# A scheduled attention and mixing kernel: a new order of the same operations, and two warm-up matmuls placed earlier

## The chip, the cores and the metric

The kernel runs on one core of a Trainium2 chip. The metric is the device time of the whole program in microseconds (us). A core has a matmul engine (PE, with its weight loads listed as PEld), a vector engine (DVE), a scalar engine (ACT), a general engine (POOL), and a queue (SP) from which this kernel issues all its DMAs.

## What is computed

Four batches of 768 positions go through block-sparse attention with 8 heads of 64 columns: each query sees its neighbours at a distance under 16 and 24 summaries of blocks of 32 keys (the largest key, the mean value). The 512 output columns of a position then go through a rotation by an angle that they set themselves, two 768x768 mixes over positions, and a 512x512 channel product:

```python
k_sum = k.reshape(B, H, nb, block, D).max(axis=3)
v_sum = v.reshape(B, H, nb, block, D).mean(axis=3)
scores = concat(where(abs(i - j) < 16, scale * q @ k.T, -1e9), scale * q @ k_sum.T + log(32))
x = softmax(scores) @ concat(v, v_sum)            # (4, 768, 512) after the heads are joined
theta = x @ w_theta
zr, zi = x * cos(theta), x * sin(theta)
u = x + w_tok_r @ zr + w_tok_i @ zi               # over positions, per batch
out = u + maximum(u @ w_ch, 0)
```

The weights arrive as 8-byte floats and are turned into 4-byte floats on the chip by integer operations on DVE.

## The kernel before

`attn_moe` records 2292 operations (a few instructions each) with their readers and writers; nothing is decided while they are recorded. `Program.schedule` then walks the table `ORDER`: each word is the number of an operation, and a letter behind it (`d` DVE, `g` POOL) says on which engine it goes, where it may go on several; without a letter it goes to the engine with the smallest cost. The instructions are issued in this one order, so the table sets the order on every engine's queue and on SP, and the waits follow from the data. Every engine works its own queue in order and waits where its next instruction's data or buffer isn't there.

The parts that are spoken of below, with their lines:

- Warm-up (`K["WARM"]`, lines 374 to 379): five matmuls of a 128x512 tile of zeros into the bank `t`, whose result nobody reads. In the trace each is two pieces of L379.
- `prepass` (L446, L450): block maxima of the keys (`ks`, DVE) and, in batch 0, the value sums as matmuls of a 0/1 table with the loaded values (`x<-vn`) into `pa` on PE.
- `att_tile` for each of 24 tiles of 128 positions (6 in a batch): loads of the queries `q` (two buffers), the keys `k`, the values `v` (four buffers), scores (L523, `s`), mask and maximum (L559, DVE), exponentials (L563, ACT), transposes (L572), copies of these (L578), the value product (L546, `pa`), and the division by the sum (L587 to L596).
- `turn_tile` and `theta_tile`: a transpose (L605) and the product with `w_theta` (L639 in the first batch's six tiles, L644 later), both in the one bank `t`; the angle is reduced on ACT and DVE (L655, L657), turned into cosine and sine on ACT (L667, L668), and multiplied with `xn` in two halves (L674, on DVE or POOL, `zu`).
- `mix_step` (L702, batches 0 and 1) and `mix_fast` (L817, batches 2 and 3, seven products instead of eight; four of them read sums of weights that `weight_sums` has put into `s_scratch`, loaded by `wt<-s_scratch`).
- `out_batch` (L922 and the lines around it): the channel product, in seven products again.

Exponential and sine stand in different tables of ACT; where one follows the other, an ACT_TABLE_LOAD is issued between them.

```python
for word in ORDER.split():
    o = self.ops[int(word.rstrip("padg"))]
    o.eng = dict(p="PE", a="ACT", d="DVE", g="POOL").get(word[-1]) or min(o.cost)
    order.append(o)
```

Of the kernel before, what the change touches and what calls it, by code (L numbers as in the profile page):

```python
# [54 lines left out]
17g 8 0g 1g 31 23 27 25 9 24 18 29 10 28 2 26 39 3 19 32 30 20 4 44g 33 5 6g 190g 49g 46 45 48 7 50 86 194g 47 193 51 60 61 34  # L55
35 52 53 79 191 64 239g 192g 87 57 55 62 54 66 13 88 65 185 11 93 14 42 238 63 89 12 36 241g 40 90 59 58 240g 91 100 67 56 80
195 37 38g 235 68 15 92d 188 186 81 69 107 21 82 204 94 71 205 206 108 41g 43d 70 83 209 290 207 95g 187 72 109 84 237 210 196
208 199 76 295g 198 73 197 294g 200 189g 74 77 22 242 203 96 101 75d 102g 201 202 78d 236 251 252 351g 254 212 211 103 213 97
253 104 85 98 215 214 110 223 216 296g 258 224 99d 225 243 255 257 217 118 348g 226 105 227 218 119g 220d 293 256 245 219d 106
244 246 228 247 250 111 120 221 291 121 249 222d 248 123 124g 297 229 122 349g 298 345 259 230 260 262 292 299 261 270 130 125  # L60
301 350g 115 300 271 263 126 272 303 423g 305 302 304 306 273 267d 308 131g 307 116 264d 419 310 135 268 309 265 274 313 127
136g 132 311 312 266d 141 275 269d 314 276 133 315 142g 137 317 316 277 138 352 143 112 231 325 326 318 232 134 327 163 233g
139 144 353 361 168 319d 356 328 320 329 362 278 330 322 355 234 169g 145 331 346 164g 321d 279 364 323 363 282 117 146 324
283 420 332 354 113 347 284 280 365 474 285 147 380 358 114 357 339 165 360 148 366 359 337 166 367 338 149 167 170 368 150
152 381 424 369 422 333 370 400 153 382 128 383 384 171 334 154 172 155 157 281 158g 156 425 385 371 402 401 159 372 386 340
174 335 175g 373 426 392 394 374 421 160 375 377 376 378 387 529 161 404 176 388 379 403 705g 389 454 177 530 179 395 393 178
180 455 456 390g 472 408 457 181 405 182 410 183 427 703 458 459 414 466 409 412 460 461 462 463 411 435 428 467 429 704g 406
437 706g 438 415 431 430 441 468 615g 469 413 436 434 464g 707 521 442 433 465 432 416 417 407 479g 440 564d 523 443 439 480
288g 741 709g 534 444 446d 418 481 535 482 445 485 483 447 490 477 129 492 491 484 475 448 478g 493 486 496 449 451d 532 710g
452 743 450d 488 531g 522 453d 497 616g 487 536 509 537 539 494 586 476d 540 489 538 495 498 510 621 499 391g 501 543 500d 541  # L70
742 511 502 512 545 503 506 513 542 547 551 504 546 733 507 583 289g 286g 708g 549 505d 550 533g 343g 548 544 745 508d 514 744
552 553 515 341 554 555 524 516 556d 517 711 712 518 287g 713d 714 739 585 336g 557 344g 398 734 587 596 558d 599 519 624 588
603 559 715 592 589 716 746 717 561 668 568 591 562 565g 622 735 593 718 566 719 584 560d 597 140 601 720 595 563 598 567 600
602 399g 784 590 594 623 342 569 785d 604 473g 721 786 740 605 572 625 607d 570 634 606 576 608 626 635 787g 617 788 653g 722
618 665 638 151 789 629 574 697 637 630 396d 397g 470 619 525g 723g 737 639 627 790 698g 609d 620 636 628 520 832 612 633 736
471g 162 641 833g 654g 659g 613 738 834g 631 791 640 610 611d 632 792 614d 655 841 642 747 752 643 835g 669 526 644d 793 645
670 646 812 678 672 657 679 650 813d 671 173 667 683 681 658 814d 815 680 663 647d 836 673 748 842 816 675 664 684 843g 817
656 648 818 755 754 724 945g 837 674 682 844 819 660g 677 661 649d 651 666 527d 652 676 685 820 686 687 794 839 689 821 688d
795 838g 756 1015 757 690 528g 571 845g 975 765 662 822 759 760 976d 850 691 840 977d 578 846 978 851g 796 768 823 727d 763
184 797 852 946 699 766 758 692 853g 769 1020 701 694d 979 940 702 980 700 941 847g 772 848 693d 579 981 825 767 695 749 696d  # L80
761 762 771 731 753 750 764 580g 798d 824 982 728 770 732 773 983 774 775d 984 947 956 581g 776 854g 777 995 948 729 778d 959
849 781d 949 950 958 725g 582g 802 952 803 996 997 998 953 799g 859 751 943 1016 1021 779 951 782 855 999 730 780 1074 1000
985 860g 1001 856 800 726 963 1018 808 857 1002 942 954 861g 957 961 960 962 801 955 575 826g 783 964 862 863g 1077 858 944g
965 1003 1022 966 1004 986 967d 864g 968 1005 806 804 1017g 810 1031 972 868 805 865g 1050 828 1023 1051d 1052 1032 869g 573
577 987 829 1170 1053 830 1024 866 1025 1033 989g 1006 969d 1054 827 1035 1037 831 1029 1055 870 1028 993 871 1056 1007g 970
872g 1027 1034 867 973 1120d 1038 1008 877 994 1036 1026 1057 1019d 1058 1013 1030 971 1014 974d 873d 1059 1039 874g 1040 1042
1078 878 1041d 809 811 990g 1079 1043 1047d 1208 1076 807 1087 1089 991 876 992 1209 1088 1090 1011 1210d 1083 1094 1093 1044d
1060 879 1009 880 1211 1080 1212 875 881 1082 1129 1012 1045 882g 1048 1213 886 1061 1126 1081 1092 1066 883 1075 1010 884
1084 1091 1214 1063g 1085 887 1067 885 1062 1127 1121 1046d 988 888 1215 1086 1173 1068 1049 1216 895 1095 1096 1098 1106g
1130 1217 1097d 889 1099 1218d 1279 1107g 1280 1281g 1069 1131 1070 896 1071 1228 1133 1100d 1282 1064g 1219 1135 890 1103d  # L90
1229 1283 1072 1073 1139 1065 891g 1137 1132 1110 1141 892 1142 1101 1284 1111 897 1143 1104 1285 1134 1138 1102d 898g 1108
1105d 1145 899g 1146 1286 1140 1144 1136 1109 1287 1128 893 900d 1158d 1147 1148 901g 1150 894 1288 1172 1250 1149d 1118 1174
1289 1114 1175 1112 1151 1305 1116 1178 1179 902 1202 1236 1122 1152 1183 903 1221g 1123 1306 1124 1185 1307 1308g 1187 1177
1181 1309 1153 904 1182 1160 1184 1232 1310 1155 1189 1237 1230 1233 1220g 1188 1176 1125 1186 1311 905 1156 1162 1171 1290
1312 906g 1249 1154 1163 1203 1247 1190 1180 1157 1234 1313 1159g 1191 1192 1193 1291g 1231 1251 1314 1222g 1194d 907 1315d
1252 1254 1195 1235 1292g 1117 1354 1240 1196 1253 1355 1260 1261 1356 1161 1199d 1255 1357g 1166 1168 1319 1197 1358 1198d
1322 1256 1257 1241 1258 1164d 1165g 1169 908g 1316 1263 1242 1200 913 1359 1206 1264 1360 1259 1207 1201d 1243 909 1324 1361
1167 1262 1248 1317g 1267 1382 1599g 1266 1268 1265 1362 1269 910g 1325 1326 1363 1271d 911 1364d 1270 1327 1272 16 1368 1600g
1335 1238 1204 1226 1330 1369d 914g 1328 1463 1370d 1365 915 1387 1276 1371 1366 1205 1367g 912 1273d 1331 1334 1372 1224 1338
916 1595g 1373 1225 1274 1337 1239 1383 1587g 1374 1223 1329 917 1385 1275 1244 918g 919 1245 1293 1596g 1277 1375 1376 1227  # L100
1278 1377 1588g 1333 1388 1320 920 1332 921 1589d 1246g 1339 1294 1297 1321d 1384 1378d 1417 931 1336 1295 1342 1296 1418 1341
1419g 1323 1420 1389 922 1672 1340 1593 1301 1594 1113 1119 1343 923g 1590 1318g 1344 1644 1346 932g 1421 924g 1345 1302 1646
# [1020 lines left out]
```

## Time and profile before

| | |
|---|---|
| time, median of 3 runs | 435.23 us (433.77 to 435.77) |
| the profiled execution | 437.3 us, its span 435.6 us |
| PE busy | 421.7 us, 97% of the span |
| DVE, ACT, POOL busy | 81%, 64%, 48% |
| DMA | 100.07 MB, mean 230 GB/s |
| the chain of work that ended last | PE 87%, DMA 10%, DVE 1%, ACT 1% |

Busy time is read as time in which an instruction of the engine is under way. The span runs from the first instruction to the last; 1.7 us of the profiled execution lie outside it.

### The profile page before, as it was taken

Reading aid. Unit: us, or ns where it says so; the run is one execution under the profiler, and the core shown is the slowest. Engines: PE = TensorE matmul, PEld = TensorE weight load, DVE = VectorE, ACT = ScalarE, POOL = GpSimd, SP = SyncE. Lnnn points to the kernel's source line nnn. Section 1 sums busy time; section 2 is a strip of 40 time slices with the busy share of each in tenths; the row PEclk is TensorE's granted clock in tenths of the full one; section 3 lists DMA queues with packets and bytes.
Section 4 is the critical chain, followed back from the end, with each engine's and each line's share of the span. In section 5 each row is a group of like instructions: output and inputs, shape, how many; then the busy total and the mean of one; then the engine's idle time right before and its main releaser. Section 6 shows DMA issues by size and latency. Waiting matters only on the chain.

```text
span 435.6 us, 10044 instructions
## 1 busy us (share of the span) xinstructions
PE 421.7 (97%) x3682; PEld 350.9 (81%) x3682; DVE 352.2 (81%) x947; ACT 280.3 (64%) x600; POOL 209.7 (48%) x208
## 2 busy tenths in 40 slices
PE   5989999998999999999999999999999989999996
PEld 1455555665888888888888899999899989999996
DVE  3799999778988777875757695866489989999996
ACT  1799995787757784866785885493955447455210
POOL 3543324687775665245465578624453410251542
PEclk9899999999999999999999999999999999999999
DMA  8999956989678678848767987883379696220138
GB/s 294 347 354 364 295 197 208 290 257 322 230 233 273 197 224 266 259 139 247 232 188 223 292 273 218 245 246 119 111 230 338 229 367 223 75 73 20 65 136 289
DMA packets 76321, 100.07 MB, mean 230 GB/s; under 512 B 23024, under 2 KB 58864, under 8 KB 76272
## 3 DMA queue, kind: packets, MB, share of 16 engines
q1 hardware_dynamic: 76272, 99.43, 71.1%
q8 instruction: 29, 0.48, 0.5%
q14 instruction: 20, 0.16, 0.1%
HBM read 75.82 MB, written 23.59 MB: 228 GB/s over the span
## 4 chain that ended last, share of the span: by engine, by line
PE 87%; DMA 10%; DVE 1%; ACT 1%; SPq 0%; issue 0%; POOL 0%; DVEq 0%
PE m L702 25%; PE m L817 19%; PE t L644 11%; PE c L922 7%; PE m L922 6%; PE pa L546 5%; PE s L523 4%; PE t L639 3%; PE t L605 3%; DMA q<-qg 3%; PE pa L572 3%; DMA wth<-wth 2%; DMA wt<-wti 2%; DMA zu<-kT 2%; DMA wt<-s_scratch 1%; PE t L922 1%
## 5 line engine op out<-in xcount | busy, mean ns | idle before, releaser
L817 PE MATMUL m<-wt,hl 128*128 128x384 f32 x504 | 95.7, 339 | 1.4 <-DMA wt<-s_scratch 1.2
L817 PEld LDWEIGHTS m<-wt,hl 128*128 128x128 f32 x504 | 87.7, 188 | 4.9 <-ACT hl L309 1.5
L702 PE MATMUL m<-wt,hl 128*128 128x512 f32 (+1 forms) x432 | 84.9, 341 | 0.0
L702 PEld LDWEIGHTS m<-wt,hl 128*128 128x128 f32 x432 | 68.6, 188 | 10.8
L563 ACT ACTIVATE e<-e,st 128x118 f32<-128x118 f32 x192 | 63.1, 388 | 12.1 <-DVE st L559 11.6
L559 DVE CUSTOM_DVE_ANT_0 e<-s,cs 128x118 f32<-128x118 f32 x192 | 46.8, 272 | 9.6 <-PE s L523 4.7
L318 POOL TENSOR_TENSOR hl<-zu,hl 128x512 fp32r<-128x512 f32 x23 | 30.1, 1309 | 43.9 <-DMA wt<-s_scratch 15.9
L644 PE MATMUL t<-wth,xh 128*128 128x512 f32 x144 | 45.3, 396 | 0.0
L674 POOL TENSOR_TENSOR zu<-xn,zu 128x512 f32<-128x512 f32 x20 | 27.0, 1350 | 20.3 <-ACT zu L668 5.5
L657 DVE SCALAR_TENSOR_TENSOR zu<-zu,t 128x512 f32<-128x512 f32 x24 | 16.4, 684 | 24.4 <-ACT zu L655 24.4
L702 PE MATMUL m<-wt,zu 128*128 128x512 f32 (+1 forms) x96 | 33.4, 491 | 1.2 <-DVE zu L674 1.2
L655 ACT ACTIVATE zu<-t,bmagic 128x512 f32<-128x512 f32 x24 | 16.5, 687 | 23.9 <-PE t L644 18.3
L309 ACT CAST hl<-zu 128x512 fp32r<-128x512 f32 x31 | 19.1, 619 | 18.2 <-PE m L817 14.9
L702 PEld LDWEIGHTS m<-wt,zu 128*128 128x128 f32 x96 | 17.5, 190 | 15.8 <-issue 12.6
L546 PEld LDWEIGHTS pa<-v,e 118*64 118x64 f32 x768 | 24.8, 137 | 6.8 <-issue 3.0
L318 DVE TENSOR_TENSOR hl<-zu,hl 128x512 fp32r<-128x512 f32 x37 | 27.6, 751 | 2.3 <-ACT hl L309 2.1
L523 PE MATMUL s<-k,q 64*64 64x118 f32 x768 | 25.6, 272 | 3.9 <-POOL cs L340 3.2
L546 PE MATMUL pa<-v,e 118*64 118x65 f32 x768 | 28.1, 224 | 1.2 <-ACT e L578 1.2
L730 POOL TENSOR_TENSOR zu<-zu 128x512 f32<-128x512 f32 x15 | 21.4, 1432 | 15.0 <-DVE zu L730 4.9
L644 PE MATMUL t<-wth,xl 128*128 128x512 f32 x72 | 28.6, 397 | 0.0
L674 DVE TENSOR_TENSOR zu<-xn,zu 128x512 f32<-128x512 f32 x28 | 24.7, 884 | 4.8 <-ACT zu L668 4.6
L523 PEld LDWEIGHTS s<-k,q 64*64 64x64 f32 x768 | 20.2, 135 | 9.2 <-POOL cs L343 4.0
(181 smaller groups left out, 909.9 us busy)
## 6 DMA issues: line engine op xcount, KB each, us to landing
wt<-s_scratch SPq DMA_DIRECT2D x48, 384.0 KB, 4.4
v<-vg SPq DMA_DIRECT2D x48, 195.0 KB, 5.3
s_scratch<-f SPq DMA_DIRECT2D x24, 384.0 KB, 3.9
k<-kg SPq DMA_DIRECT2D x18, 376.0 KB, 5.5
q<-qg SPq DMA_DIRECT2D x24, 256.0 KB, 6.0
wt<-wtr SPq DMA_DIRECT2D x6, 768.0 KB, 11.0
wt<-wti SPq DMA_DIRECT2D x6, 768.0 KB, 11.4
f<-kT SPq DMA_DIRECT2D x12, 384.0 KB, 4.3
```

The lines of the kernel that those rows point to most:

```text
L309: nc.scalar.copy(dst(), src())
L318: lambda e: V[e].tensor_tensor(dst(), src(), hi().bitcast(F32), op=ALU.subtract), reads, writes, due, port=BOTH)
L523: mm(0.79 * len(pairs) / NP, [lambda p=p, g=g, h=h: nc.tensor.matmul(sc[h].get()[ROW[g], p], q.get()[ROW[h], p, ROW[g]], k.get()[ROW[h], p ...
L546: mm(2 * 0.433 + scores[0] + (0.2 if scores[0] else 0.0), [lambda n=n, g=g, a=a: nc.tensor.matmul(xa[a].get()[ROW[g], n], turned[g].get()[ ...
L559: op({"DVE": 0.205}, lambda eng, n=n: nc.vector.tensor_tensor_reduce(e()[:, n], sc[n % 2].get()[:, 2 * a + n // 2], mask(m), -SCALE, 3.0e3 ...
L563: op({"ACT": 0.288}, lambda eng, n=n: nc.scalar.activation(e()[:, n], e()[:, n], AF.Exp, bias=st.get()[:, n:n + 1], scale=-1.0), [(st, n)] ...
L644: calls = [lambda t=t, xx=xx, k=k, c=c: nc.tensor.matmul(th.get(), xx.get()[:, c], w_th[c].get()[:, k], start=(c == 0 and t == 0), stop=(c ...
L674: op({"DVE": c_dve(DM, "two"), "POOL": c_pool(DM)}, lambda e, z=z, hc=hc: V[e].tensor_tensor(z(), xn[b, i].get().rearrange("p h d -> p (h ...
L702: nc.tensor.matmul(acc[th](), zz, w[:, TT[th]], start=(s == 0 and r == 0 and t == 0 and (th == 0 or c == 0)), stop=(s == NT - 1 and r == 1 ...
L730: lambda e: V[e].tensor_tensor(dst(), x(), y(), op=ALU.add if sign > 0 else ALU.subtract), reads, writes, due, port=BOTH)
L817: calls = [lambda ref=ref, tt=tt, z=z, s=s, j=j, t=t, x=x, k=k, bank=bank, first=first: nc.tensor.matmul(bank[j].get()[:, :HT], z.get()[:, ...
L922: calls = [lambda k=k, t=t, x=x, y=y: nc.tensor.matmul(to.get(), weights[n][x][0]()[:, k, j * P:(j + 1) * P], operands[n].get()[:, y, k], ...
```

## The change

Only the table `ORDER` differs; the 2292 operations, their costs, buffers and sizes are the same, and the file after is one line shorter, so that its line numbers are one lower. 267 operations go to another engine than before (of those that may choose), and of the 548 operations on PE 208 keep their place in PE's queue while the rest move, by 21 places at most and by 1.6 in the mean.

```diff
 ORDER = """
-17g 8 0g 1g 31 23 27 25 9 24 18 29 10 28 2 26 39 3 19 32 30 20 4 44g 33 5 6g 190g 49g 46 45 48 7 50 86 194g 47 193 51 60 61 34
...
+17g 23 25 8 9 24 18 31 19 21 22 27 0 11 28 29 26 1g 2 10 3 30 44 48g 46 4 45g 32 49 39 5 47g 33 190 6 20 50 7g 51 191g 60 86
...
```

In the table, 17 is the memset of the zeros, 18 to 22 are the five matmuls on them, and 32 is the first value sum.

**PE, the start of the program.** `t<-zu` are matmuls on zeros (two of them stand as x2), `pa<-x,vt` the value sums of batch 0, `s<-k,q` the scores of tile 0. Before:

```order
L379 MATMUL t<-zu 128x512 x2
L450 MATMUL pa_107<-x,vt 24x512 x2
L379 MATMUL t<-zu 128x512
L523 MATMUL s_129<-k,q 64x118
L523 MATMUL s_131<-k,q 64x118
```

After:

```order
L378 MATMUL t<-zu 128x512 x4
L449 MATMUL pa_117<-x,vt 24x512 x2
L378 MATMUL t<-zu 128x512
L522 MATMUL s_132<-k,q 64x118
L522 MATMUL s_134<-k,q 64x118
```

Two matmuls on zeros stand ahead of the first value sums now; before they stood behind the transposes and behind the value product of tile 0. On SP the first value load `x<-vn` goes third instead of first, behind two of the four key loads.

**SP, the 25th DMA and its neighbours.** `wt` are the mixing weights, `q` the queries of tile 4, the `v` ahead of and behind it the two halves of tile 3's values. Before:

```order
L303 DMA wt<-wti 128x1536
L303 DMA wt<-wtr 128x1536
L303 DMA v<-vg 96x520
L303 DMA q<-qg 128x512
L303 DMA v<-vg 96x520
```

After:

```order
L302 DMA wt<-wti 128x1536
L302 DMA wt<-wtr 128x1536
L302 DMA q<-qg 128x512
L302 DMA v<-vg 96x520 x2
L302 DMA wt<-wtr 128x1536
```

The queries of tile 4 stand ahead of both halves of tile 3's values now.

**PE, and the engine that makes its input, at the last mix step of batch 0's first half.** `t<-wth,..` is the angle of tile 6, `m<-wt,zu` the mix of tile 5. PE before:

```order
L644 MATMUL t<-wth_972,xh 128x512 x2
L644 MATMUL t<-wth_972,xl 128x512
L702 MATMUL m_722<-wt,zu 128x512
L702 MATMUL m_704<-wt,zu 128x256
L644 MATMUL t<-wth_1011,xh 128x512 x2
L644 MATMUL t<-wth_1011,xl 128x512
L702 MATMUL m_702<-wt,zu 128x512
```

DVE before, where `zu<-xn,zu` makes the half of tile 5 that this mix reads:

```order
L588 TENSOR_SCALAR st<-pa_1271 128x4
L559 ISA e,st<-s_1296,cs 128x118
L559 ISA st 128x1
L674 TENSOR_TENSOR zu<-xn,zu 128x2x256
L559 ISA e,st<-s_1294,cs 128x118
```

PE after:

```order
L643 MATMUL t<-wth_923,xh 128x512 x2
L643 MATMUL t<-wth_923,xl 128x512
L643 MATMUL t<-wth_987,xh 128x512 x2
L643 MATMUL t<-wth_987,xl 128x512
L701 MATMUL m_686<-wt,zu 128x512
L701 MATMUL m_688<-wt,zu 128x256
L701 MATMUL m_721<-wt,zu 128x512
```

POOL after, where the row with x2 makes both halves of tile 5:

```order
L317 TENSOR_TENSOR wth_987<-xl,wth_987 128x512
L494 COPY v<-vs 24x520
L317 TENSOR_TENSOR wt<-wt 128x768
L673 TENSOR_TENSOR zu<-xn,zu 128x2x256 x2
L317 TENSOR_TENSOR wt<-wt 128x768 x2
```

The fourth group of the angle of tile 6 stands ahead of the mix now, and tile 5's product moved from DVE to POOL.

ACT's queue holds 28 table loads before and 36 after. Before, the sines of tiles 9 and 10, 16 and 17, 18 and 19, 20 and 21 shared one load; now each tile has its own, and as many loads lead back to the exponentials.

## Rows read from the trace of the kernel before

**Rows 1.** The page, part 1: engine, busy us, share of the span, instructions.

```profile
PE 421.7 (97%) x3682; PEld 350.9 (81%) x3682; DVE 352.2 (81%) x947; ACT 280.3 (64%) x600; POOL 209.7 (48%) x208
```

**Rows 2.** Stages: length, busy PE, PEld, DVE, ACT, POOL, clock, DMA share, GB/s.

```profile
40.00:100.00 60.00, 58.63 (x518) 35.43 (x510) 53.57 (x144) 50.47 (x107) 28.80 (x28) 1.00 0.81 258
100.00:160.00 60.00, 60.00 (x639) 49.42 (x639) 49.08 (x155) 42.78 (x99) 41.45 (x38) 1.00 0.75 244
160.00:240.00 80.00, 80.00 (x763) 68.30 (x762) 55.87 (x185) 55.10 (x119) 39.42 (x38) 1.00 0.75 226
...
300.00:340.00 40.00, 40.00 (x258) 37.73 (x258) 30.48 (x63) 23.33 (x51) 19.91 (x17) 1.00 0.60 201
340.00:430.00 90.00, 88.58 (x506) 87.64 (x505) 87.04 (x140) 38.35 (x64) 27.88 (x18) 1.00 0.45 154
```

**Rows 3.** Waits of PE: who waited for whom, us in total, times, longest.

```profile
PE m L702 <- DVE zu L674: 1.2, 1, 1.2
...
PE m L817 <- DMA wt<-s_scratch: 1.2, 1, 1.2
PE t L605 <- DVE zu L657: 0.7, 1, 0.7
PE s L523 <- DMA q<-qg: 0.4, 1, 0.4
```

**Rows 4.** PE in order of time at the start: start, us, what, idle before.

```profile
1.39 3.40 PE L379 MATMUL t<-zu 128*128 128x512 f32 x4 [1.39 <-POOL zu L377]
4.72 1.90 PE L450 MATMUL pa<-x,vt 128*24 128x512 f32 x4
...
10.92 1.78 PE L523 MATMUL s<-k,q 64*64 64x118 f32 x32 [3.25 <-POOL cs L340]
12.63 4.53 PE L450 MATMUL pa<-x,vt 128*24 128x512 f32 x8
17.09 1.04 PE L523 MATMUL s<-k,q 64*64 64x118 f32 x32
...
18.66 1.12 PE L379 MATMUL t<-zu 128*128 128x512 f32 x2
```

**Rows 5.** Short stretches of the start, columns as in rows 2.

```profile
10.90:12.60 1.70, 1.68 (x32) 1.43 (x32) 0.06 (x1) 0.84 (x4) 1.49 (x6) 0.56 1.03 404
14.85:17.10 2.25, 2.25 (x9) 0.43 (x7) 2.16 (x7) 2.07 (x7) 1.58 (x3) 1.00 1.06 340
```

**Rows 6.** The chain that ended last, its first 40 us: start, us, what.

```profile
18.58 9.06 DMA wt<-wti
...
27.66 11.64 DMA q<-qg
```

**Rows 7.** SP's queue, the issue ahead of that of tile 4's queries.

```profile
26.87 0.33 SPq L303 DMA_DIRECT2D v<-vg  x1
```

**Rows 8.** ACT on the way to the first mix.

```profile
41.10 0.59 ACT L309 COPY x<-t 128x512 f32<-128x512 f32 x1 [0.40 <-PE t L605]
```

**Rows 9.** ACT and DVE around the wait at 99 us, in order of time.

```profile
96.98 0.62 ACT L668 ACTIVATE zu<-zu 128x512 f32<-128x512 f32 x1
...
97.50 0.81 ACT L309 CAST wt<-wt 128x768 fp32r<-128x768 f32 x1
...
97.62 2.30 DVE L674 TENSOR_TENSOR zu<-xn,zu 128x512 f32<-128x512 f32 x1
...
98.33 1.28 ACT L563 ACT_TABLE_LOAD   x1
```

**Rows 10.** POOL in the same stretch.

```profile
96.30 1.30 POOL L674 TENSOR_TENSOR zu<-xn,zu 128x512 f32<-128x512 f32 x1 [1.58 <-DVE xl L318]
```

**Rows 11.** PE in the same stretch.

```profile
97.90 0.62 PE L644 MATMUL t<-wth,xh 128*128 128x512 f32 x2
...
99.98 1.56 PE L702 MATMUL m<-wt,zu 128*128 128x512 f32 x4 [1.23 <-DVE zu L674]
```

**Rows 12.** PE at 351 us.

```profile
351.48 1.80 PE L817 MATMUL m<-wt,hl 128*128 128x384 f32 x9 [1.20 <-DMA wt<-s_scratch]
```

More of the change, by code (lines that the diff above doesn't have):

```diff
@@ L59 @@
[L59 to L66, printed above, removed]
@@ new lines @@
+612 638 622 396d 832 727g 630 637 665 609d 629 788 618 833g 628 789 627 574 619 790 613 745 632 610 639 633 631 611d 641 744
+620 636 791 614d 728g 755 162 640 724 657 642 746 397 792 643 793 645 644d 739 669 646 678 681 812 655 834g 670 747 472 672
+673 658 666 682 835g 740 173 813 473g 841 794 659g 647d 940 471 656 814 815 679 650d 816 674 654g 677 676 817 671 667 818 648
+661 651 836g 819 685 680 663 752 748 683 675 753 649d 945g 652 686 837d 526 684 842g 687 660 795 820 688d 756 689 697 757 690
@@ new lines @@
+946 821 759 843g 975 765 691 976d 796g 838g 844 662 694d 527 528 692 839 664 701 797 699 693d 749 822 578g 702 768 845g 767
+823 766 977 763 771 769 760 978 840 846 979 764 698 731 825 943 571 850 750 579 941 758 980 981 732 751g 695 696 982 851g 852g
+762 847 848 770 761 1020 772 754 580d 700 773 983 853 824 1021 798 849 774 581g 775d 984 854g 947 776 956 777 582g 1018 995
+781d 802 958 948 949 950 957 944 959 778d 996 855g 729 859 997 1015 951 985d 856g 963 960 730 998 954 953 860g 725d 962 779
@@ new lines @@
+1059 1079 1009g 874g 807 1043 878g 1080 1087 879g 1208 1082 1047 811 1209 1084 1210 1014 880g 1090 875 876 1068 1076 886 1091
+1044d 1048 1045 1094 1211g 991 1008g 1060 1212 992 1213 1086 1083 1061 1046 1063g 1173 1089 1081 1069 881 882d 887g 1214 1049
+1010g 1011 1093 1088 1085 883g 1092 888g 1215 1012 884 1095 889g 885 1096 895 1130 1097d 1062g 1216 1098 1099 1131 1217 1103
+1279 1139 1280d 1218 1141 1104 1140 1135 1281 1072 1066 1282g 1132 1144 1067 1143 1228 1106g 890g 896g 1133 1283 1070 1120g
@@ new lines @@
+1335 1327 1276d 1370 1273d 1277 1205 913 1224 1371g 1388 1372 1274 1238 1275d 1338 1278 1337 1239 1223g 1225 1373 1364 1365
+912 1600g 1227 1385 914 1330 1329 1374 1366g 1367 1375 1244 1341 922 1331 1593d 1376 1463 923 915 1328 1377 924g 1293 1383
+1339 1333 1603g 1295 1342 1589g 1320 1336 1334 1434 1245 1340 1378 925g 916g 1417 1418 1294 1246 1389 1419d 1297 1332 1323g
+1590 917g 1343 1119 1344 1296 1420 1301 1379 1303 1345 1421 918 1422 1390 1346 1644 1681 1298 1595d 1321d 1393 1380g 1394 1423
@@ new lines @@
+1424 1347 1397 1425 1299 1594g 1645 1351 1431 1647 1391 919 1649 1386g 1658 1646 1426 1395 1648 1675 1381 1596g 1660 1398
+1348d 1384d 920 1651 1427 1352 1349 1399 1302 1662 1428 1401 1405 1350d 1650 1353d 926g 1678 1403 1400 1402 1392 1396 1404
+1429 1591g 1115 927d 1435 1592 1406 1407 1652 928 921 1653 1409 1408d 1611 1597 1654 931 1436 1598 1300 1410 1411 1672 1604g
+1527 1304 1664 932g 1437 930 1656 929 1444 1439 1430 1528 1659 1498 1529 1655 1661 1446 933 1447 1601 1663 934 1432 1530 1451
@@ new lines @@
+1580 1686 1473 1692 1619g 1701 1462 1689 1620g 1612 1540 1484 1485 1539 1499 1581 1613 1617d 1618g 1623g 1582 1486 1487d 1691
+1488 1766 1690 1627 1614g 1500 1508 1583d 1489 1767 1694 1697 1693 1511 1696 1502 1768g 1492 1493 1769 1621d 1512 1501 1699
+1504 1700 1584 1509 1704 1513 1497 1506 1770 1729 1510 1703 1771 1707 1490 1503 1622 1632 1507 1732 1491 1496 1629 1702 1624
+1625g 1505 1772 1705 1706 1494d 1735 1773 1585g 1709 1628 1514 1774 1738 1708 1586g 1515 1516 1517 1626 1775 1518 1543 1519d
@@ L141 @@
+2258 2262 2264 2282 2263 2268 2285 2265 2280 2289 2228 2283 2266 2269 2286 2284 2267 2287 2259 2270 2288 2290 2291
 """
```

136 lines of the change are left out of this document (59 added, 77 removed).

## The prediction

> **What bounds the kernel now.** First the page's list of engines: PE is busy for 421.7 of 435.6 us [rows 1], so what is left for any order to win is 13.9 us, and the question is where these lie. The table by stages gives that: from 40 us on PE has no idle slice but in two stages, 40 to 100 (58.63 of 60) and 340 to 430 (88.58 of 90); from 100 to 340 it is full in every stage shown, and this at a granted clock of 1.00 [rows 2]. PE's work is the same in both kernels, so after 40 us only waits of PE can be won, or made. The list of waits names them: 1.2 us of the mix L702 for DVE's product `zu` and 1.2 us of L817 for a load of `wt<-s_scratch` [rows 3]. Two more of that list stand before 40 us: 0.7 us of a transpose for DVE's L657, and 0.4 us of scores for a load of `q`.
>
> Before 40 us it is another program. PE waits 3.25 us ahead of its first scores [rows 4], and the loads share the 16 DMA engines at 1.03 and 1.06 of their time [rows 5]: they pace the start. The chain of waits says so too: up to 39.30 us it goes from load to load, the last one that of tile 4's queries, issued at 27.66 and landed after 11.64 us [rows 6]. That issue comes 0.02 us after the weights `wti` issued at 18.58 have landed (18.58 + 9.06 = 27.64): SP issues when an earlier load has landed.
>
> **The two matmuls on zeros.** An operation of them is two pieces. At the start four pieces took 3.40 us, 0.85 each, and behind the transposes one operation took 1.12 [rows 4], so the two taken out of there free about 2.2 us of PE between 18 and 23 us. Put in at the start they cost 4 x 0.85 = 3.40 us at most; PE there has an idle 3.25 us to fill, and ends its early work at 10.92 or at worst (1.39 + 3.40 + 3.40 + 1.90 + 1.12 = 11.21) some 0.3 us behind it. The second gain is speed. The scores that follow the idle stretch ran at a granted clock of 0.56, a mix of the two levels 1.2 and 2.4 GHz [rows 5], and took 1.78 us where the same 32 matmuls take 1.04 at 17.09; the eight pieces of value sums behind took 4.53 where four took 1.90, that is 4.53 - 3.80 = 0.73 too much [rows 4]. If PE isn't idle before, up to 0.74 + 0.73 = 1.47 us come back. So PE gains 2.2 + 1.47 = 3.7 us of room, and I count none of it: PE then waits longer for the loads of tile 2 to 4, which land when they did [rows 6]. What hides the edit is the DMA pace; the bounds are 0 and -3.7, and the row that it is nearest to is the chain's, hence 0. The first value load goes third rather than first on SP; the sums that read it now start 3 us later, so nothing is late by that.
>
> **Queries of tile 4 ahead of tile 3's values.** The issue moves from 27.66 to the place of the `v` at 26.87 [rows 6, 7], 0.79 us earlier; by bytes, one `v` of 96x520 4-byte numbers is 199.7 KB, at 340 GB/s [rows 5] an estimated 0.59 us. So PE's scores of tile 4 start 0.59 to 0.79 us earlier, more than their wait of 0.44. How much of it arrives at the first mix? The way there goes through ACT, which copies tile 4's turned columns at 41.10 and was idle for 0.40 us only ahead of that [rows 8]; the ACT work in front of the idle time hangs on weights' landings that don't move. So **-0.40**, between 0 and -0.79. The values of tile 3, delayed by one load of `q`, are read by PE behind the scores and land before them.
>
> The Trainium skill's page "DMA: Bandwidth & Descriptors" (section "Queues, rings and completion order") says that transfers issued by one engine need not complete in the order of issue; by that an earlier issue buys nothing sure, this term could be 0 and the time 434.0. In this trace the issue that follows a landing by 0.02 us speaks for the order of issue at the start.
>
> **Tile 5's product from DVE to POOL, and the angle's fourth group ahead of the mix.** ACT ends the sine of tile 5 at 96.98 + 0.62 = 97.60; DVE takes the product at 97.62 and needs 2.30 us [rows 9], to 99.92, and PE's mix starts at 99.98 after 1.23 us idle [rows 11], so that it was ready at 98.75. After the change POOL makes it. POOL's own product in this stretch took 1.30 and POOL had been idle for 1.58 us before it [rows 10]; from 97.60 it is done at 98.90. PE arrives later than before, by the group that now stands ahead (three pieces; the last such group ahead of the mix began at 97.90, so one takes 98.75 - 97.90 = 0.85) [rows 11]: 98.75 + 0.85 = 99.60. That is 0.70 us behind POOL, so the wait is gone: **-1.23**. With POOL at 2.30, as slow as DVE was, it would be 99.90, a wait of 0.30 and a gain of 0.93. The angle's group costs nothing, since it only trades places. The second half of tile 5, which POOL makes next (to 100.20), has its mix much later.
>
> **The wait at 351.** PE's queue is the same there, and so is the distance in PE's work from the issue of the `wt<-s_scratch` loads to the mix that waits [rows 12]; I leave it, 0, with bounds -1.20 (gone) and +1.20 (twice as long).
>
> **Eight more table loads.** One takes 1.28 us [rows 9]. Eight are 10.3 us of ACT, and where they stand ACT is busy for 42.78 of 60, 55.10 of 80 and 23.33 of 40 us [rows 2], that is idle for 17.2, 24.9 and 16.7 us. That is the cover: 0 on PE's path, at worst all 10.3. The 12 operations more on ACT and 11 fewer on DVE that the new letters bring go the same way; DVE, busy for 87.04 of 90 us at the end [rows 2], is relieved if anything. Elsewhere PE's moves, 1.6 places in the mean, change no work: 0, with a new wait as a rival below.
>
> The page "ScalarE: Activation LUTs" of the Trainium skill (section "What ACT_TABLE_LOAD costs") adds a drain to the load, some 2.66 us for a switch, 21 us for eight. The trace shows none: the cast ends at 97.50 + 0.81 = 98.31, the load starts at 98.33 [rows 9]. By the page the slower rival below would be twice as dear.
>
> **The sum.** -1.23 - 0.40 = -1.63 us. Made against the profiled run that is 437.3 - 1.6 = 435.7 (its span 435.6 and 1.7 us around it); that run lies 2.1 above the median of the three, so on the median: 435.23 - 1.63 = **433.6**.
>
> **Rivals.**
> 1. More is won. The wait at 351 goes with the transfers around it (-1.20), the transposes at the start no longer wait for DVE (-0.68), and the queries bring their whole 0.79 instead of 0.40 (-0.39): -2.27 beyond the forecast, 431.3. For it: all are small and hang on orders that changed. Against it: PE's order is unchanged at the first, and the other two are bounded by the loads.
> 2. A new wait of the old size. One of the products that move to POOL, where it takes 1.27 to 1.30 against 0.7 of DVE undisturbed, is what a mix of the next tiles waits for, as the mix of tile 5 did for 1.23: 433.6 + 1.2 = 434.8, the gain of the start alone. For it: 267 operations change engines, and 340 of PE's 548 change place. Against it: from 100 us on the mixes never waited for these products.
> 3. Slower: the table loads. Where a tile's sines split two runs of exponentials, the scores of the next tile wait in `e` for ACT, and PE for its transposes. If of the four pairs two lie on PE's path, four loads of 1.28, 5.1 us, are paid: 433.6 + 5.1 = 438.7; with all eight 443.9. It decides when a tile's stretch leaves ACT less than one pair (2.6 us) idle. For it: ACT is the engine whose order this change worsens most. Against it: some three tenths to two fifths of ACT's time is idle in those stages.
> 4. That the order doesn't do what it says is excluded in the queues; at the start it does it with no effect if the loads pace everything, which is the 0 already taken.
>
> **How the numbers follow.** A measurement of this kernel can tell about 0.5%, 2.2 us: faster is under 433.05, slower over 437.4. The three runs differ by 2 us, so a forecast of 433.6 lies on both sides of the first bound. Forecast (432.4 to 434.6): 0.40, of it 0.17 faster and 0.23 same. Rival 1: 0.25, of it 0.24 faster and 0.01 same. Rival 2: 0.19, of it 0.01 faster, 0.15 same, 0.03 slower. Rival 3: 0.16, of it 0.02 same and 0.14 slower. Sums: faster 0.42, same 0.41, slower 0.17. The range 430.5 to 437.5 leaves out a fifth of rival 1 (0.05), most of rival 3 (0.13) and the end of rival 2 (0.02).
>
> **What would show it.** In the profile of the changed kernel: no idle time of PE ahead of the mix of tile 5 near 98 to 99 us, POOL's L673 at 1.3 us behind the sine; the scores of tile 0 at 1.04 us and a granted clock of 1.00 at 11 us; yet the scores of tile 4 near 39 us, 0.4 to 0.8 earlier; the same wait for `wt<-s_scratch` near 350; 36 table loads with PE full from 100 to 340 us. I am wrong if PE shows idle time in that stretch with ACT as its releaser (rival 3), if a mix waits for POOL (rival 2), or if the first mix of batch 0 starts 2 us or more earlier, for then the DMA pace wasn't what bounded the start.

## The result and the profile after

The changed kernel takes 441.18 us (median of 4 runs, 439.32 to 441.72) against 435.29 us of the kernel before (433.77 to 435.77): a ratio of 1.0133, with a 95% interval of 1.0106 to 1.0160. It is slower by 5.9 us by these medians, where 433.6 and a range up to 437.5 had been forecast.

The page of the kernel after, part 1, answers to [rows 1]:

```profile
PE 422.5 (96%) x3682; PEld 350.1 (80%) x3682; DVE 353.8 (80%) x936; ACT 299.1 (68%) x629; POOL 205.6 (47%) x207
```

PE has the same work (422.5 us busy, 421.7 before), in a span of 440.0 instead of 435.6 us: the loss is waiting. Its place is read from the waits of PE of the kernel after (columns as in [rows 3]; the line numbers are one lower than before):

```profile
PE pa L545 <- ACT e L577: 2.2, 2, 1.2
PE s L522 <- POOL k L499: 2.1, 3, 1.4
PE m L816 <- DMA wt<-s_scratch: 1.6, 3, 0.9
...
PE pa L449 <- DMA x<-vn: 1.2, 1, 1.2
PE s L522 <- DVE st L558: 1.0, 1, 1.0
PE m L701 <- DVE x L720: 1.0, 1, 1.0
...
PE s L522 <- ACT f L400: 0.6, 1, 0.6
```

All of these but the L816 and L701 rows belong to the first 45 us. The mix that waited 1.23 us for tile 5's product (L702 for `zu`) is no longer in the list. Two rows of PE, the scores of tile 4 and the first mix, say when the start is over:

```profile
42.24 1.04 PE L522 MATMUL s<-k,q 64*64 64x118 f32 x32 [0.62 <-ACT f L400]
...
48.71 1.56 PE L701 MATMUL m<-wt,zu 128*128 128x512 f32 x4
```

The same two in the kernel before:

```profile
39.44 1.04 PE L523 MATMUL s<-k,q 64*64 64x118 f32 x32 [0.44 <-DMA q<-qg]
...
45.65 4.57 PE L702 MATMUL m<-wt,zu 128*128 128x512 f32 x13
```

They stood 2.80 and 3.06 us earlier. So three of the 4.4 us by which the span grew are lost in the start. Three stretches of the start, of the kernel before (first three rows) and of the kernel after (last three), columns as in [rows 2], the last two being the DMA share and GB/s:

```profile
3.00:8.00 5.00, 4.67 (x9) 0.97 (x7) 1.07 (x2) 0.00 (x0) 0.56 (x2) 1.00 1.00 369
8.00:20.00 12.00, 8.87 (x90) 3.98 (x90) 9.84 (x40) 8.56 (x22) 5.26 (x13) 0.86 1.04 368
20.00:38.00 18.00, 16.02 (x218) 9.98 (x218) 16.80 (x74) 17.38 (x45) 9.64 (x15) 1.00 1.04 344
```

```profile
3.00:8.00 5.00, 4.42 (x7) 1.54 (x5) 1.18 (x3) 0.00 (x0) 1.33 (x4) 1.00 0.93 340
8.00:20.00 12.00, 9.21 (x88) 3.27 (x90) 7.75 (x30) 6.58 (x19) 4.64 (x14) 1.00 1.04 347
20.00:38.00 18.00, 13.27 (x224) 9.05 (x219) 15.80 (x72) 15.98 (x41) 12.03 (x17) 1.00 1.03 317
```

From 8 us on the DMA engines are as full as before (1.03 to 1.04 of their time), and move less: 347 and 317 GB/s instead of 368 and 344. The chain of waits of the kernel after, in its first 45 us, goes from load to load again:

```profile
5.82 11.93 DMA wth<-wth
17.77 9.89 DMA v<-vg
27.68 13.49 DMA wt<-wtr
```

The last one is the 26th load, a block of the mixing weights; it lands at 27.68 + 13.49 = 41.17. In the kernel before the 26th load is the same block, behind the same 25 loads in another order, and it lands at 37.65. The profile puts the 0.62 us ahead of the scores of tile 4 down to ACT, which takes the first step of turning this block into floats there (L400, done at 42.11). But the scores read `k` and `q`, and the queries of tile 4, now the 27th load, are issued here:

```profile
28.48 0.33 SPq L302 DMA_DIRECT2D q<-qg  x1
```

They land at 42.11, and the scores start 0.14 us behind that, exactly as in the kernel before (landed at 39.30, scores at 39.44). So it is these queries that PE waits for in both kernels, and they come 2.8 us later although they stand one place earlier.

### The profile page after: what moved, and what is told of

It is laid out like the page before. It is cut to its first block, busy times and chain, and to the rows that moved or that the text cites. A ratio compares the mean times of both kernels' runs of the same rounds, so it can differ in the third digit from the quotient of the medians.

```text
span 440.0 us, 10050 instructions
## 1 busy us (share of the span) xinstructions
PE 422.5 (96%) x3682; PEld 350.1 (80%) x3682; DVE 353.8 (80%) x936; ACT 299.1 (68%) x629; POOL 205.6 (47%) x207
## 4 chain that ended last, share of the span: by engine, by line
PE 80%; DMA 14%; SPq 2%; DVE 2%; ACT 0%; issue 0%; DVEq 0%
PE m L701 23%; PE m L816 18%; PE t L643 9%; PE c L921 7%; PE m L921 5%; PE pa L545 5%; DMA wt<-s_scratch 4%; PE s L522 4%; PE t L638 3%; DMA wt<-wtr 3%; DMA wth<-wth 3%; PE t L604 3%; PE pa L571 2%; DMA v<-vg 2%; SPq L302 2%; DMA f<-f_scratch 2%
## 5 line engine op out<-in xcount | busy, mean ns | idle before, releaser
L816 PE MATMUL m<-wt,hl 128*128 128x384 f32 x504 | 95.6, 339 | 1.7 <-DMA wt<-s_scratch 1.6
L816 PEld LDWEIGHTS m<-wt,hl 128*128 128x128 f32 x504 | 87.6, 188 | 6.0 <-DMA wt<-s_scratch 2.5
L701 PE MATMUL m<-wt,hl 128*128 128x512 f32 (+1 forms) x432 | 85.2, 341 | 1.0 <-DVE x L720 1.0
L701 PEld LDWEIGHTS m<-wt,hl 128*128 128x128 f32 x432 | 68.4, 188 | 12.2 <-DVE x L720 1.6
L562 ACT ACTIVATE e<-e,st 128x118 f32<-128x118 f32 x192 | 64.0, 390 | 6.4 <-DVE st L558 4.6
L673 POOL TENSOR_TENSOR zu<-xn,zu 128x512 f32<-128x512 f32 x23 | 31.1, 1358 | 23.2 <-ACT zu L667 11.6
L701 PE MATMUL m<-wt,zu 128*128 128x512 f32 (+1 forms) x96 | 33.3, 491 | 0.0
L308 ACT CAST hl<-zu 128x512 fp32r<-128x512 f32 x33 | 20.1, 620 | 15.9 <-PE m L816 11.3
L317 DVE TENSOR_TENSOR hl<-zu,hl 128x512 fp32r<-128x512 f32 x38 | 30.1, 795 | 0.9 <-POOL hl L310 0.5
L577 DVE COPY e<-pa 118x512 f32<-118x512 f32 x17 | 11.7, 690 | 23.6 <-PE pa L571 23.4
L729 POOL TENSOR_TENSOR f<-f 128x192 f32<-128x192 f32 x31 | 20.0, 647 | 19.7 <-DVE f L729 9.9
L522 PE MATMUL s<-k,q 64*64 64x118 f32 x768 | 25.3, 268 | 3.8 <-POOL k L499 2.1
L701 PEld LDWEIGHTS m<-wt,zu 128*128 128x128 f32 x96 | 17.4, 190 | 13.9 <-issue 12.1
L577 ACT COPY e<-pa 118x512 f32<-118x512 f32 x31 | 17.5, 587 | 14.2 <-PE pa L571 14.2
```

The costliest lines, as they stand in the source:

```text
L308: nc.scalar.copy(dst(), src())
L317: lambda e: V[e].tensor_tensor(dst(), src(), hi().bitcast(F32), op=ALU.subtract), reads, writes, due, port=BOTH)
L522: mm(0.79 * len(pairs) / NP, [lambda p=p, g=g, h=h: nc.tensor.matmul(sc[h].get()[ROW[g], p], q.get()[ROW[h], p, ROW[g]], k.get()[ROW[h], p ...
L562: op({"ACT": 0.288}, lambda eng, n=n: nc.scalar.activation(e()[:, n], e()[:, n], AF.Exp, bias=st.get()[:, n:n + 1], scale=-1.0), [(st, n)] ...
L577: lambda e, t=t, g=g: (nc.scalar.copy if e == "ACT" else nc.vector.tensor_copy)(t.get()[:NK], tp[g].get()[:NK].rearrange("k n q -> k (n q) ...
L673: op({"DVE": c_dve(DM, "two"), "POOL": c_pool(DM)}, lambda e, z=z, hc=hc: V[e].tensor_tensor(z(), xn[b, i].get().rearrange("p h d -> p (h ...
```

## The experiments

Fourteen kernels were run. The runs of before and of each kernel were made on one chip side by side; each ratio is to the before of its own group (medians 435.28 to 435.44). A ratio is taken over the runs that are compared and is not the quotient of the two medians; the two can differ by 0.1% (`weights_first`: 1.0037 and 1.0048), so that the intervals decide. Nearly every kernel here is a table `ORDER` put together from the two tables, so that the diffs show words of the table, cut to those that move.

### Which part of the program loses it

`before_start` takes the table of before up to the first mix, then what is left in the order of after; `after_start` the other way round.

```diff
 before_start
-(all words of before)
+(the first 295 words of before) (the other words, as they follow in after)
 after_start
-(all words of before)
+(the first 284 words of after) (the other words, as they follow in before)
```

> The order of the kernel before up to the first mix of batch 0 (its first 295 table entries), the rest in the order of the kernel after. Theory (the loss is made at the start, by loads that move fewer bytes in a microsecond: the scores of tile 4 start at 42.24 instead of 39.44): the first mix starts near 45.65 as before, the +3.05 us of the start are gone, what the rest makes by PE's waits is -1.4 (tile 5's product) +1.4 (L701 at 114 us) +0.9 (L816 at 296) -0.1 (351), so 435.3 + 0.8 = about 436.1. Rival (the loss is in the later waits): 438 to 440.

> The order of the kernel after up to the first mix of batch 0 (its first 284 table entries), the rest in the order of the kernel before. Theory (the start makes the loss): the first mix starts near 48.7, 3 us late, the rest keeps its waits, 435.3 + 3.0 = 438.3. Rival (later waits): within 1 us of 435.3.

`before_start`: 436.29 us, ratio 1.0029 (1.0008 to 1.0049). `after_start`: 438.72 us, 1.0088 (1.0065 to 1.0112). The two parts make 1.0117 together, within the interval of the whole change (1.0106 to 1.0160); three quarters of these 1.17% are the start. The PE rows of `before_start` (first two) and of `after_start`:

```profile
38.51 1.04 PE L523 MATMUL s<-k,q 64*64 64x118 f32 x32 [0.78 <-DMA q<-qg]
44.74 5.43 PE L702 MATMUL m<-wt,zu 128*128 128x512 f32 x16
```

```profile
41.87 1.04 PE L523 MATMUL s<-k,q 64*64 64x118 f32 x32
48.09 2.42 PE L702 MATMUL m<-wt,zu 128*128 128x512 f32 x6
```

### The kernel before once more

> The kernel before, unchanged, for its spread. If the speed of the loads at the start differs from execution to execution, the packets of the values (2080 bytes, median 118 ns between 20 and 40 us in the first profile of before, 147 in that of after) and the start of tile 4's scores (39.44) differ here by more than 1 us from the first profile; the theory that the order decides expects them within 0.5 us, and a ratio of 1.000 +- 0.002.

435.21 us, ratio 0.9994 (0.9976 to 1.0012). Its profiled execution had the scores of tile 4 at 38.72 (39.44 in the first profile), the 26th load at 37.39 (37.65), and 335 GB/s between 20 and 38 us (344). So two executions of one order differ by 0.7 us at this place; the two of after's start, 42.24 and 41.87, lie 2.4 to 3.5 us behind both. The expected 0.5 us was too narrow, the theory stands. A second thing differs by execution: the wait for `wt<-s_scratch` at 351 us. It was 1.20 us in the profile on which the prediction rests [rows 12]; here PE shows none:

```profile
343.71 8.56 PE L817 MATMUL m<-wt,hl 128*128 128x384 f32 x44
352.49 0.76 PE L817 MATMUL m<-wt,hl 128*128 128x384 f32 x3 [0.22 <-DVE x L826]
```

### The two matmuls alone

```diff
-... 3 19 32 30 20 ... 21 ... 22 ...
+... 3 19 21 22 32 30 20 ...
```

(18 to 22 are the matmuls on zeros, 32 the first value sum.)

> The kernel before with the two matmuls on zeros moved ahead of the first value sums and nothing else. Theory (the order of the loads makes the loss, the matmuls are in PE's idle time): the scores of tile 0 at 1.0 to 1.2 us instead of 1.78, the first mix within 0.5 us of 45.65, 435.3 +- 0.7. Rival (the matmuls delay the start themselves): the first mix 1 to 3 us late, 436.3 to 438.3.

435.68 us, ratio 1.0016 (1.0001 to 1.0031): at most a small loss. In its profiled execution, the longest of its twelve (437.79 us), the scores of tile 0 took 1.33 us (1.78 in the first profile, 1.36 in that of `before_again`), those of tile 4 began at 39.61, the first mix at 45.83. What names the change in its headline is not what costs the time.

### The order of the loads alone

`before_loads_after` is the kernel before with its first 29 loads in the order of after; `after_loads_before` is the kernel after with its first 29 loads in the order of before.

```diff
-31 23 27 25 29 39 33 86 35 79 185 93 42 40 100 235 188 186 107 108 290 109 237 236 110 111 291 345 292
+23 25 31 27 29 39 33 86 35 79 185 42 40 93 100 235 107 186 188 108 290 109 237 236 110 111 345 291 292
```

(31, 29 and 33 are the first values, 23 to 27 and 39 keys and queries, 86, 79, 93 and 100 `wth`, 42 and 40 the halves of tile 0's values, 188 and 186 those of tile 1, 107 and 108 the first blocks of `wtr` and `wti`, 345 the queries of tile 4, 291 and 292 the values of tile 3.)

> The kernel before; only the first 29 loads are issued in the order of the kernel after (the same 29 loads), every other engine keeps its order. Theory A (the order of the loads makes the start slow: the third block of weights of wtr, the 26th load in either order, lands at 41.17 in after, 37.4 to 38.2 in three executions with the start of before): that landing near 40, the scores of tile 4 near 41.5, 435.3 + 2 to 3 = 437.3 to 438.3. Rival B (the order of ACT, DVE and POOL at the start makes it slow, and the loads follow, since an issue waits for buffers): the scores of tile 4 at 39 to 40, 435 to 436.

> The kernel after; only its first 29 loads are issued in the order of the kernel before. Theory A: the scores of tile 4 come back to 39 to 40, 441.2 - 2 to 3 = 438 to 439 or lower. Rival B: they stay near 42, 440.5 to 441.5.

`before_loads_after`: 439.19 us, 1.0085 (1.0051 to 1.0119). `after_loads_before`: 436.53 us, 1.0031 (1.0008 to 1.0054). The order of 29 loads, with nothing else changed, makes as much as the whole start (1.0088), and with the old order of loads the kernel after loses no more than it does with the whole old start. The stretch from 20 to 38 us, and in a fence of its own the row of the scores of tile 4, of `before_loads_after` (first two fences) and of `after_loads_before` (last two):

```profile
20.00:38.00 18.00, 14.04 (x210) 8.91 (x212) 15.11 (x66) 14.66 (x36) 7.81 (x13) 1.00 1.04 331
```

```profile
43.09 1.04 PE L523 MATMUL s<-k,q 64*64 64x118 f32 x32
```

```profile
20.00:38.00 18.00, 16.46 (x199) 10.18 (x194) 16.99 (x72) 16.95 (x45) 10.07 (x16) 0.91 1.03 351
```

```profile
38.60 1.04 PE L523 MATMUL s<-k,q 64*64 64x118 f32 x32
```

The landings of three loads in the traces, in us from the start of the span, say where the time goes. The sets of loads up to each are the same in all kernels (`weights_first` and the others below are the single moves):

```
order of the loads         kernel               11th    16th    26th
before                     before               16.5    22.7    37.6
                           before_again         15.6    21.2    37.4
                           before_start         15.7    20.9    37.1
                           warm_only            16.1    21.6    38.2
                           after_loads_before   15.2    20.0    36.6
after                      after                18.6    23.6    41.2
                           after_start          17.3    21.5    39.5
                           before_loads_after   18.7    24.5    41.7
before, one move           weights_first        15.4    20.0    37.5
                           values_early         15.5    20.1    36.8
                           keys_first           15.9    22.1    38.7
                           q4_first             15.3    20.0    36.8
```

The executions profiled of `after`, `before_loads_after` and `warm_only` were the longest of their kernels; that of `after_start` (438.98 us) stands in the middle of its six, and its 26th load still lands 1.4 us behind the latest of the old order. One thing holds in all 16 traces: none of the 9th to the 30th load is issued before the load eight places ahead of it has landed, and most of them 0.02 to 0.08 us behind that. So a load that lands late also delays the issue eight places on, and in this way the order of the first loads reaches the later ones.

### The moves one by one

```diff
 weights_first
-235 188 186 107 108
+235 107 188 186 108
 values_early
-185 93 42 40 100
+185 42 40 93 100
 keys_first
-31 23 27 25 29
+23 25 31 27 29
 q4_first
-111 291 345 292
+111 345 291 292
```

> The kernel before with one load moved by two places: the first block of wtr goes ahead of the two halves of tile 1's values instead of behind them (loads 17 to 19), as in after. The 17th to 19th load together took 3.1, 4.0 and 4.4 us from landing to landing in three executions with the start of before, 4.8 and 5.6 us in two with that of after. Theory A in its narrow form (this group makes half of the loss): the three take 5 us or more and the scores of tile 4 start 1.0 to 1.5 later than in before, 436.3 to 436.8. Rival: 3.5 to 4.4 us, and 435.3 +- 0.5.

437.38 us, ratio 1.0037 (1.0012 to 1.0063). The three loads took 5.3 us and the scores of tile 4 came at 40.30, 0.9 us behind the first profile and 1.6 behind `before_again`, about as theory A expected, but the way there was another: the 26th load is not late (37.5), and these scores don't wait for their queries, which land at 38.84. What is late are the values themselves: with 768 KB of weights ahead of them they land at 24.6 and 25.3, where the later half came at 24.1 in before and 22.5 in `before_again`, and PE's value product of tile 1 waits for them. First of the waits of PE:

```profile
PE pa L546 <- DMA v<-vg: 2.2, 1, 2.2
```

In this execution the wait has a second price. Behind it the granted clock of PE is 0.51 from 26.0 to 29.4 us, nearly all of that at the lower of its two levels (1.2 GHz instead of 2.4). The value product and the matmuls behind it, here and (last two rows) in the kernel before, where PE had waited 0.66 us and the clock was 1.00:

```profile
25.44 1.76 PE L546 MATMUL pa<-v,e 118*64 118x65 f32 x32 [2.20 <-DMA v<-vg]
27.12 2.08 PE L639 MATMUL t<-xh,x 128*128 128x512 f32 x2
```

```profile
25.70 1.22 PE L546 MATMUL pa<-v,e 118*64 118x65 f32 x32 [0.66 <-ACT e L578]
26.85 1.13 PE L639 MATMUL t<-xh,x 128*128 128x512 f32 x2
```

From the start of the value product to the third of these pairs PE takes 4.60 us instead of 2.97, so that the slow stretch costs 1.6 us on top of the wait. Not every wait is followed by one: in `keys_first`, below, PE waits 1.67 us and its scores then take 1.04 us as always.

> The kernel before with the two halves of tile 0's values loaded 12th and 13th instead of 13th and 14th, ahead of a block of wth, as in after. Theory (values beside a large block make the loads slow): the 11th load lands 0.7 to 1.3 us later than the 15.1 to 16.5 of the runs with before's loads, the 26th near 38, 435.3 + 0.5 to 1. Rival: nothing, 435.3 +- 0.4.

435.94 us, 1.0020 (1.0005 to 1.0035): the time is in the expected band, the reason isn't: neither the 11th nor the 26th load is late. The execution profiled is the shortest of its twelve (435.41 us), so where the loss lies isn't seen.

> The kernel before with the first two loads of keys ahead of the first load of values, as in after. In two executions of the start of after the third load landed 2.4 to 3.4 us behind the second, in seven with before's loads 1.1 to 2.4. Theory (this place costs about 0.6 us, since all loads follow one another): 435.3 + 0.6. Rival (the third landing varies by itself): 435.3 +- 0.4.

437.87 us (median of seven runs; an eighth, 441.89, is not in the ratio), 1.0055 (1.0030 to 1.0081), and widely spread, 435.21 to 439.77. Much dearer than the 0.6 us expected. The first value sum waits for its values (first row), and the queries of tile 4 are late (second row, the scores of tile 4); the chain of waits up to these goes through loads alone:

```profile
7.36 1.88 PE L450 MATMUL pa<-x,vt 128*24 128x512 f32 x4 [2.19 <-DMA x<-vn]
...
40.28 1.04 PE L523 MATMUL s<-k,q 64*64 64x118 f32 x32 [1.67 <-DMA q<-qg]
```

The profiled execution (436.97 us) is among the faster ones of this kernel, so that what its slower ones do isn't seen.

> The kernel before with one load moved by one place: the queries of tile 4 go ahead of the first half of tile 3's values, as in after. This is the term of the prediction that was put at -0.40 (between 0 and -0.79). By the prediction: these queries land 0.6 to 0.8 earlier against the 26th load, 434.9. By the theory that has come out of the runs (a load's place changes the speed of the loads around it): the values of tile 3 stand side by side then, the loads around lose what the queries gain, 435.3 +- 0.4.

435.63 us, 1.0000 (0.9986 to 1.0013). In the trace the queries of tile 4 land 0.8 us behind the 26th load, where in the other executions of the old order they land 1.2 to 1.7 behind it: they are earlier by 0.4 to 0.9 us, as forecast. Their scores start at 37.68 and the first mix at 44.40, which is hardly outside what the old order shows by itself (37.96 to 39.61 and 44.22 to 45.83). By time no gain of the 0.4 us forecast can be told from none.

In time the first three moves make 0.37 + 0.20 + 0.55 = 1.12%, the whole order 0.85% (0.51 to 1.19): they are enough for it. That their losses add up in this way isn't shown: part of that of `weights_first` is the lower clock, and the granted clock of the kernel after is 1.00 from 8 to 38 us. By landings they don't add up: the 26th load lands at 39.5 to 41.7 with all moves and at 36.8 to 38.7 with any one. Why they slow the loads more together than alone stays open.

### Is it the place of the values in memory?

```diff
-dma(lambda g=g: v[g].get()[NB:], lambda g=g: vg[b, 2 * i + g], ...
+dma(lambda g=g: v[g].get()[NB:], lambda g=g: vg[b, 2 * i + g][:, :H * DV].rearrange("p (h d) -> p h d", h=H), ...
...
-vg = np.zeros((B, NG, VL, H, DV), np.float32)
+vg_rows = np.zeros((B, NG, VL, 640), np.float32)
```

> The kernel before with the values stored in rows of 2560 bytes instead of 2080, of which 2080 are loaded as before. The packets of the values (2080 bytes) take 85 ns at best, 118 to 132 in the median between 20 and 40 us, and the packets of the weights beside them (6144 bytes) rise from 234 to over 300. If this comes from the place of the rows in memory, both fall towards 85 and 235 here, the start is paced less, and the time is 432 to 434. If it comes from where the rows are written or from the number of rows (96 for 16 engines), nothing changes: 435.3 +- 0.5.

435.47 us, ratio 0.9992 (0.9973 to 1.0011): no change by itself. In the trace a packet of the values takes 112 ns in the mean between 8 and 38 us here, 120 and 129 ns in the two executions of before, 146 in that of after; 85 is its least. Rows 2560 bytes apart don't bring the packets back to that, so their place 2080 bytes apart is not what slows them.

### Tile 5, and the late waits, alone

```diff
 tile5_only
-... 344g ... 519 ... 568 ... 718 566 ...
+... 519g 344g ... 718 568 ... 566 ...
 late_only
-(all words of before)
+(the words of before up to PE's 304th operation) (the other words, as they follow in after)
```

(519 is the product of tile 5, 344 a subtraction on POOL, 718 the angle's last group, 568 the mix.)

> The kernel before with two changes near 98 us and none elsewhere: the half of tile 5's product that the mix waits for goes on POOL, ahead of a subtraction (L318) that POOL does there, and the last group of the angle of tile 6 stands ahead of that mix. Theory (this term of the prediction was right): the wait of 1.23 to 1.26 us ahead of that mix is gone, 435.3 - 1.2 = 434.1. Rival (something later swallows it): 435.3 +- 0.4.

434.80 us, ratio 0.9982 (0.9962 to 1.0002). PE ahead of the mix, in `before_again` (first row) and in `tile5_only` (the angle's last group and, with no idle time, the mix):

```profile
99.18 1.56 PE L702 MATMUL m<-wt,zu 128*128 128x512 f32 x4 [1.24 <-DVE zu L674]
```

```profile
97.78 0.62 PE L644 MATMUL t<-wth,xh 128*128 128x512 f32 x2
98.23 0.40 PE L644 MATMUL t<-wth,xl 128*128 128x512 f32 x1
98.47 1.88 PE L702 MATMUL m<-wt,zu 128*128 128x512 f32 x5
```

The wait is gone; of the 1.2 us the medians show 0.6, and the interval just reaches no gain. In the traces PE is 1.5 us ahead of `before_again` behind this mix, loses 0.4 of it near 106 us and 0.2 near 142, and keeps 0.9: the rival, that something later swallows the gain, is right in part.

> The order of the kernel before up to PE's 304th operation (some 265 us), the rest in the order of the kernel after. The kernel with before's start and after's rest ran 436.3 although the wait at tile 5 is gone from it, so that some 2 us are lost behind. Theory (PE's waits near 283 and 345 to 352 us, for the loads of the sums and DVE, make this loss): 435.3 + 1.5 to 2.5 = 436.8 to 437.8, waits of 0.5 us or more near 283 and 1 us or more near 350. Rival (it is lost between 100 and 265 us): 435.3 +- 0.5.

436.15 us, 1.0012 (0.9996 to 1.0027): less than expected, and not sure to be a loss. The trace has the waits near 350 that were expected (two of 0.9 us), and none near 283:

```profile
345.74 4.94 PE L817 MATMUL m<-wt,hl 128*128 128x384 f32 x27 [0.91 <-ACT hl L309]
351.57 1.68 PE L817 MATMUL m<-wt,hl 128*128 128x384 f32 x8 [0.89 <-DMA wt<-s_scratch]
```

The order of after behind the start costs 1.0029 although it has the gain at tile 5 in it; what makes this is settled only in part: some of it lies here, the rest in small waits that differ from run to run.

### What helped, together

```diff
-the words of before, rows of 2080 bytes
+the words of tile5_only, rows of 2560 bytes
```

> The kernel before with the two changes near 98 us (tile 5's product on POOL, the angle's last group ahead of the mix) and with the values in rows of 2560 bytes. If both small effects are real (0.9982 and 0.9992 alone), 435.3 x 0.9974 = 434.2; the rows alone were within their interval of no change, so 434.2 to 434.8.

434.17 us, ratio 0.9967 (0.9952 to 0.9983): faster than both kernels, by 1.2 us and by about 7. The interval overlaps that of `tile5_only` (0.9962 to 1.0002), so what the rows add to it isn't shown.

## Why the prediction was wrong, step by step

- **Tile 5's product, -1.23: right.** In the kernel after POOL begins the two halves 0.07 us behind the sine (99.92 + 0.62 = 100.54), and the mix follows the angle's last group without idle time. Rows of ACT, POOL and PE of the kernel after, answering to [rows 9 to 11]:

```profile
99.92 0.62 ACT L667 ACTIVATE zu<-zu 128x512 f32<-128x512 f32 x1
...
100.61 2.83 POOL L673 TENSOR_TENSOR zu<-xn,zu 128x512 f32<-128x512 f32 x2 [3.42 <-ACT zu L667]
...
102.23 2.31 PE L701 MATMUL m<-wt,zu 128*128 128x512 f32 x6
```

Here the kernel after makes up 1.5 us of its lateness in the traces (2.94 us late ahead of this stretch, 1.44 behind it). Alone it is worth 0.6 us by the medians (0.9982, with 1.0002 at the end of the interval).

- **The order of the loads, -0.40: this is the step that failed.** I costed one moved load, the queries of tile 4, and took the others to land when they did. Three more had moved: keys ahead of the first values, tile 0's values ahead of a block of `wth`, a block of weights ahead of tile 1's values. Put together the order of the 29 loads costs 1.0085, some 3.7 us, and in the kernel after the queries of tile 4 land at 42.11 instead of 39.30 and their scores come 2.80 later, not 0.4 to 0.8 earlier. Two sentences of the prediction hold the mistake: that the loads "land when they did", and that the first value sums "now start 3 us later, so nothing is late by that"; in the kernel after they wait 1.2 us for `x<-vn` (in the list of waits above), and `keys_first` shows what this move costs alone, 1.0055. The profile had shown that the loads pace the start; the conclusion should have been that every change of their order is a change of the path, and that each moved load has two prices: that of what it delays, and that of the rate at which the loads around it run.

- **The queries' own term** was sized well by the landings: alone the queries land 0.4 to 0.9 us earlier against the 26th load. It doesn't show in the time (1.0000). The Trainium skill's page "DMA: Bandwidth & Descriptors" (section "Queues, rings and completion order"), which was weighed there, says that completion need not follow the order of issue. No trace here shows such a case: in all 16 the first 30 loads landed in the order of issue.

- **The two matmuls on zeros, 0: nearly right.** Alone 1.0016, at most a small loss. The 0.74 us of slow scores that I thought could come back was a matter of one execution: at a granted clock of 1.00, `before_again` had 1.36 us for them with the matmuls at their old place and 1.90 us of idle time ahead.

- **Eight more table loads, 0: right as far as can be seen, and the slower rival was wrong in its mechanism.** No run has them alone, but `before_start` and `after_loads_before` have all 36 and lose 1.3 us in all (1.0029 and 1.0031), not the rival's 5.1. The loads take 1283 ns each, and ACT is busier. Stages of the kernel after, answering to [rows 2]:

```profile
100.00:160.00 60.00, 58.62 (x579) 47.71 (x581) 47.59 (x152) 46.03 (x100) 32.57 (x33) 1.00 0.82 245
160.00:240.00 80.00, 79.98 (x815) 68.37 (x816) 54.96 (x175) 60.40 (x134) 46.10 (x45) 1.00 0.75 227
```

From 160 to 240 us, where ACT grew most (55.10 to 60.40 us), PE is full. From 100 to 160 it loses 1.38 us, of which 0.97 is a mix that waits for DVE's L720 and 0.3 a value product behind ACT's L308, not a table load.

- **The wait at 351 us, 0 with bounds of -1.20 and +1.20: the value was sound, the row was one draw.** The same table gave 1.20 and no wait in two executions. The kernel after has 0.88 there.

- **The rest of the order, 0: mis-sized.** With the start of before it is 1.0029, some 1.3 us, with the gain of tile 5 in it; in the trace of the kernel after the 0.97 us ahead of 115.7 us and a wait of 0.61 for `wt<-s_scratch` near 296 belong to it, and how much of it returns from run to run is open.

- **The sum and the range.** The range had no case in which the order of the loads, the one thing that the profile showed to bound the first 40 us, costs something; its only slower cases were table loads and a new wait for POOL, and of its signs of being wrong none was a later first mix, which came 3.06 us late. A part of what was needed was at hand: in the order of the loads a block of weights of 768 KB had been moved ahead of the values that PE needs next (1.0037 alone). That the loads would also move fewer bytes in a microsecond no row of before could show, and why they do stays open.

## What to carry to other kernels

Where loads pace a stretch, cost every load whose place changes, with what waits for the ones that it passes: a large block moved ahead of two small ones delays them by about its own transfer, and an engine that waits for them may run slower behind the wait (here 2.2 us of waiting and 1.6 more at the lower clock). Don't read a load's landing as fixed while the order around it changes: the same 26 loads took 36.6 to 38.2 us in one order and 39.5 to 41.7 in another. A wait taken from one profiled execution, when it is a wait for a transfer, is one draw; run the kernel before once more ahead of counting on it. And where the profile names an engine as the one that ended a wait, see whether the waiting instruction reads what that engine wrote: the scores of tile 4 were put down to ACT and waited for a load.

## What the runs showed of the hardware

- The same loads in another order moved at 317 to 331 GB/s between 20 and 38 us, at 334 to 351 in the old order, while the DMA share was 1.03 or 1.04 in both. Packets of the values (2080 bytes) took 85 ns at best, in the mean between 8 and 38 us 111 to 129 with the old order and 128 to 146 with the new one; of those of the weights beside them (6144 bytes, 234 ns at best) the slowest quarter took over 287 to 322 with the old order and over 322 to 355 with the new one. The ranges touch, so a single execution tells little.
- The third load landed between 6.5 and 8.5 us, by execution as well as by order, and later loads tend to carry that: with the old order the 26th came at 36.6 to 37.3 where the third had landed by 6.7, at 37.1 to 38.2 where it had landed at 7.0 or later.
- Behind a wait of 2.2 us on PE its granted clock was 0.51 from 26.0 to 29.4 us, and matmuls of that stretch took up to 1.8 times as long (`weights_first`: 2.08 us instead of 1.13).
- A table load of ACT took 1283 ns each time, 28 to 36 of them in a kernel.
